# Attention then SwiGLU on one core: another order of loads and work in the opening

## The chip, the core and the metric

The kernel runs on one NeuronCore of a Trainium2 chip. The metric is the device time of one execution in microseconds; a comparison uses the median over several runs. The core has a matrix engine (TensorE, PE in the profile), three engines for elementwise work (VectorE = DVE, ScalarE = ACT, GpSimd = POOL) and SyncE (SP), whose queue issues all data transfers here. Every engine works through its own instructions in order and waits on semaphores for the others. TensorE writes to PSUM, and GpSimd doesn't touch PSUM, so PSUM is read by VectorE and ScalarE alone.

## The reference: what is computed

Causal attention with a sliding window of 64 keys over 8 batches x 8 heads x 576 tokens of 64 features, and a gated feed-forward block on its result (4608 tokens, width 512, inner width 1536):

```python
scores = np.matmul(q, k.transpose(0, 1, 3, 2)) / np.sqrt(64)
rel = pos[:, None] - pos[None, :]
scores = np.where((rel >= 0) & (rel < 64), scores, -1e9)
attn = softmax(scores)                 # over the keys
x = (attn @ v), tokens x (heads * 64)
g = x @ w_gate
out = (g * sigmoid(g) * (x @ w_val)) @ w_out
```

All inputs and the output are float32 in device memory. The kernel casts to bfloat16 for the matmuls and accumulates in float32.

## The kernel before

**Tiling.** The tokens are cut into 36 groups of 128 (`ORDER`, L35). Two groups are a chunk, the unit in which q and k are loaded. Four groups (two chunks) are a tile of 512 tokens, the unit of the feed-forward. The gate and value weights are cut into six slices of 256 inner columns, `weights(s, i)` with i = 0 for gate and 1 for value; slice s serves the inner blocks m = 2s and 2s+1 of 128 columns. `weights_o(s)` loads a sixth of the output weights.

**Attention of a group.** `load` (L85) or `load1` (L95) brings q or k of a chunk, `load_vg` (L104) v of a group. `cast_k` (L122) makes bfloat16 of q or k. `turn2` (L157) transposes it by eight TensorE transposes into PSUM and copies it out to `kT` and `qT`; `turn1` (L149) does the same by two DMA transposes. `keys_before` (L133) copies the last 64 keys of a chunk in front of the next. `cast_v` (L176) makes the two shifted copies of v, `vo` and `ve`. `scores` (L196) is the product of keys and queries, with the mask added by further matmuls where `masked` is set; `weigh` (L221) is the exponential on ScalarE, followed by two VectorE multiplies with the mask where it was not set. `products` (L235) multiplies by v (a 65th column of ones gives the sum), `norm` (L251) divides, `turn_x` (L262) transposes the group's result on TensorE into `xT`, and `turn_x1` (L272) by a DMA transpose.

**Feed-forward.** `cast_w` (L287) casts a weight slice. `step(t, m, c0, n)` (L302) is block m of tile t for the n tokens from c0: four matmuls for the gate, four for the value, then tanh on ScalarE. `finish` (L317) takes the oldest open step and does its two VectorE operations, which give `hT` and release the step's PSUM. There are two PSUM buffers each for gate and value, so a step needs the `finish` of the step two before it. `project(t, s)` (L323) multiplies 128 tokens of `hT` by the output weights in 12 matmuls, evicts on ScalarE and stores. `warm(n)` (L337) issues n matmuls of zeros into a gate buffer; nothing reads them.

**What sets the order.** The kernel is written under a manual schedule: the order of calls in the source is the order of each engine's queue. The opening (L379 to L627) is a list of calls written out one by one: it does the attention of groups 0 to 11, all steps of tiles 0 and 1, the projection of tile 0, and loads all weights. From L631 a loop of regular rounds does the rest; it begins with `step(2, 0)`. A call with engines as arguments, such as `cast_k(0, "q_f", (act, dve))`, puts one half on each named engine.

**Buffers.** Two buffers each for staged q, k and v (`stage`), six for staged weights (`wst`), three each for `kT`, `qT` and the exponentials, four PSUM buffers (`ps_a`) shared by transposes, scores, products and projections. A load waits on SP's queue until its buffer has been cast; all later loads wait behind it. Eight semaphores serve the transfers in turn, so that a transfer also waits for the one eight before it.

Of the kernel before, what the change touches and what calls it, by code (L numbers as in the profile page):

```python
# [17 lines left out]
def kernel(  # L18
# [55 lines left out]
    dve, pool, act, sp = nc.vector, nc.gpsimd, nc.scalar, nc.sync  # L74
# [10 lines left out]
    def load(n, src, nm):  # L85

        x_f = stage.tile([P, H, 2, D], FP32, name=nm, tag=nm)
        ((_, b, s),) = tokens(2 * n)
        sp.dma_start(  # L89
            x_f[:].rearrange("r h c d -> r h (c d)"),  # L90
            src[b, :, s:s + 256, :].rearrange("h (r c) d -> r h (c d)", c=2),
        )
        staged[nm, n] = x_f[:].rearrange("r h c d -> r c h d")
# [28 lines left out]
    def cast_k(n, nm, eng):  # L122
        x_f = staged.pop((nm, n))
        x_b = cast.tile([P, 2, DM], BF16, name=nm + "b", tag=nm + "b")
        y = x_b[:].rearrange("r c (h d) -> r c h d", h=H)
        if isinstance(eng, tuple):
            for c in range(2):
                copy(eng[c], y[:, c], x_f[:, c])
        else:
            copy(eng, y, x_f)  # L130
        words[nm, n] = x_b
# [205 lines left out]
    def warm(n):  # L337
        w_ps = ps_f.tile([P, 512], FP32, name="w_ps", tag="g")
        for _ in range(n):
            nc.tensor.matmul(w_ps[:], wz[:, 0:P], wz[:])  # L340

    def begin():

        dve.memset(wz[:], 0.0)  # L344
        make_identity(nc, identb[:])
        dve.memset(masks[0][:], 1.0)
        dve.memset(minus[0][:], 0.0)
        pool.affine_select(
            out=masks[0][:], in_=masks[0][:], compare_op=ALU.is_ge, fill=0.0,
            base=64, pattern=[[0, 2], [1, 64]], channel_multiplier=-1,  # L350
        )
        pool.affine_select(
            out=masks[0][:], in_=masks[0][:], compare_op=ALU.is_ge, fill=0.0,
            base=-1, pattern=[[0, 2], [-1, 64]], channel_multiplier=1,
        )
        for a in range(2):

            y = minus[0][64 * a:64 * a + 64]
            pool.affine_select(
                out=y, in_=y, compare_op=ALU.is_ge, fill=NEG,  # L360
                base=64, pattern=[[-1, P]], channel_multiplier=1,
            )
            pool.affine_select(
                out=y, in_=y, compare_op=ALU.is_ge, fill=NEG,
                base=-1, pattern=[[1, P]], channel_multiplier=-1,
            )

        pool.tensor_copy(minus[1][:, 64:P], minus[0][:, 64:P])
        pool.memset(minus[1][:, 0:64], NEG)
        pool.tensor_copy(masks[1][:], masks[0][:])  # L370
        pool.memset(masks[1][0:64, 0, :], 0.0)
        for i in (0, 2):
            dve.memset(kT[i][:, :, 0:64], 0.0)
        for i in (0, 4):
            dve.memset(ve[i][0:64], 0.0)
        for x in vo + ve:
            dve.memset(x[:, :, D:VW], 1.0)

    begin()  # L379
    load(0, q, "q_f")  # L380
    load(0, k, "k_f")
    cast_k(0, "q_f", (act, dve))
    load(1, k, "k_f")
    load_vg(0)
    cast_k(0, "k_f", (act, pool))
    load_vg(1)
    warm(11)
    turn2(0, "q_f", (act, dve))
    warm(4)
    turn2(0, "k_f", (act, dve))  # L390
    cast_k(1, "k_f", (dve, act))
    warm(3)
    scores(1)
    load(1, q, "q_f")
    cast_v(0, (dve, pool, pool))
    scores(0, True)
    cast_k(1, "q_f", pool)
    load(2, k, "k_f")
    cast_v(1, (dve, None, None))
    weigh(1)  # L400
    load(2, q, "q_f")
    weigh(0)
    warm(6)
    products(0)
    load_vg(2)
    load_vg(3)
    weights(5, 0)
    load_vg(4)
    norm(0)
    keys_before(1)  # L410
    turn2(1, "k_f", (act, dve))
    warm(4)
    turn_x(0)
    turn2(1, "q_f", (act, dve))
    products(1)
    warm(1)
    scores(2, True)
    cast_k(2, "k_f", pool)
    norm(1)
    cast_k(2, "q_f", dve)  # L420
    weigh(2)
    warm(1)
    scores(3, True)
    weigh(3)
    weights(5, 1)
    load_vg(5)
    turn2(2, "q_f", act)
    load(3, k, "k_f")
    cast_v(2, (dve, pool, pool))
    keys_before(2)  # L430
    turn2(2, "k_f", dve)
    turn_x(1)
    warm(2)
    products(2)
    load(3, q, "q_f")
    norm(2)
    cast_v(3, (act, pool, pool))
    warm(1)
    scores(4, True)
    weights(0, 0)  # L440
    weigh(4)
    products(3)
    norm(3)
    cast_v(4, (act, pool, pool))
    warm(1)
    turn_x(2)
    warm(2)
    turn_x(3)
    weights(0, 1)
    scores(5, True)  # L450
    products(4)
    cast_w(5, 1, pool)
    cast_v(5, pool)
    weigh(5)
    cast_w(5, 0, dve)
    step(0, 10, 0, 256)
    norm(4)
    weights(4, 0)
    step(0, 10, 384, 128)
    turn_x(4)  # L460
    products(5)
    load_vg(6)
    finish()
    keys_before(3)
    cast_k(3, "k_f", (act, pool))
    weights(4, 1)
    norm(5)
    finish()
    step(0, 11)
    cast_k(3, "q_f", (dve, act))  # L470
    load_vg(7)
    turn_x(5)
    turn2(3, "k_f", (dve, act))
    turn2(3, "q_f", (act, dve))
    load(4, k, "k_f")
    cast_w(0, 0, pool)
    finish()
    step(1, 11, 0, 256)
    cast_w(0, 1, act)
    scores(6, True)  # L480
    load(4, q, "q_f")
    finish()
    load_vg(8)
    scores(7)
    step(0, 0)
    weigh(6)
    step(1, 0, 0, 256)
    cast_w(4, 0, pool)
    finish()
    finish()  # L490
    weigh(7)
    cast_w(4, 1, act)
    cast_v(6, pool)
    step(0, 1)
    cast_v(7, (act, pool, pool))
    products(6)
    step(0, 8)
    norm(6)
    cast_k(4, "k_f", (act, pool))
    products(7)  # L500
    turn_x(6)
    finish()
    norm(7)
    weights(3, 0)
    step(0, 9)
    cast_k(4, "q_f", (act, pool))
    cast_w(3, 0, pool)
    weights(1, 0)
    finish()
    weights(3, 1)  # L510
    weights(1, 1)
    keys_before(4)
    load_vg(9)
    finish()
    turn_x(7)
    cast_w(3, 1, pool)
    turn2(4, "k_f", (dve, act))
    turn2(4, "q_f", act)
    step(1, 8)
    finish()  # L520
    step(1, 1)
    weights(2, 0)
    load(5, q, "q_f")
    cast_w(1, 0, pool)
    finish()
    scores(8)
    cast_w(1, 1, pool)
    scores(9)
    weigh(8)
    weights_o(4)  # L530
    load(5, k, "k_f")
    step(1, 10)
    finish()
    cast_w(2, 0, pool)
    step(0, 6)
    keys_before(5)
    weights(2, 1)
    finish()
    step(1, 6)
    finish()  # L540
    step(0, 2)
    weights_o(5)
    cast_k(5, "q_f", pool)
    finish()
    weights_o(1)
    weigh(9)
    step(0, 7)
    cast_v(8, act)
    step(1, 3)
    finish()  # L550
    cast_k(5, "k_f", (act, pool))
    step(1, 9)
    cast_v(9, (dve, pool, pool))
    finish()
    cast_w(2, 1, pool)
    turn2(5, "q_f", act)
    step(0, 3)
    weights_o(2)
    load_vg(10)
    weights_o(0)  # L560
    finish()
    casts_o(1, pool)
    finish()
    step(0, 10, 256, 128)
    products(9)
    casts_o(4, pool)
    products(8)
    step(0, 4)
    norm(9)
    casts_o(5, pool)  # L570
    finish()
    finish()
    turn2(5, "k_f", act)
    cast_v(10, pool)
    load_vg(11)
    step(1, 2)
    norm(8)
    finish()
    weights_o(3)
    step(0, 5)  # L580
    load1(6, k, "k_f")
    casts_o(0, pool)
    load_vg(12)
    finish()
    scores(10)
    load(7, k, "k_f")
    scores(11)
    casts_o(2, pool)
    casts_o(3, dve)
    weigh(11)  # L590
    turn_x1(8)
    keys_before(6)
    weigh(10)
    cast_k(6, "k_f", pool)
    step(1, 7)
    step(1, 11, 256, 256)
    finish()
    turn_x(9)
    project(0, 3)
    cast_v(11, (pool, dve, act))  # L600
    load1(6, q, "q_f")
    turn1(6, "k_f")
    load1(7, q, "q_f")
    finish()
    cast_k(6, "q_f", (act, pool))
    turn1(6, "q_f")
    step(1, 5)
    products(11)
    norm(11)
    products(10)  # L610
    cast_k(7, "k_f", (dve, pool))
    step(1, 0, 256, 256)
    project(0, 0)
    norm(10)
    cast_v(12, (pool, act, act))
    turn_x(10)
    turn_x(11)
    finish()
    project(0, 1)
    load_vg(13)  # L620
    finish()
    project(0, 2)
    load_vg(14)
    keys_before(7)
    step(1, 4)
    turn2(7, "k_f", act)
    load1(8, k, "k_f")  # L627


    dve.memset(vL[:, :, :, D:VW], 1.0)  # L630
# [90 lines left out]
```

The softmax here doesn't subtract the row's maximum and nothing guards it: scores larger than these inputs give would overflow.

## Time and profile before

| | us |
|---|---|
| median of 4 runs | 339.5 |
| lowest to highest | 339.09 to 339.76 |
| profiled execution, its own time | 338.88 |
| its span, first to last instruction | 337.1 |

| engine | busy us | share of the span |
|---|---|---|
| TensorE matmuls | 328.6 | 97% |
| TensorE weight loads | 162.5 | 48% |
| VectorE | 229.1 | 68% |
| ScalarE | 150.9 | 45% |
| GpSimd | 103.0 | 31% |

The transfers moved 56.98 MB, 169 GB/s on the mean of the span; between 50 and 60 us it was 345 GB/s. To read the profile: the busy time of a matmul reaches to the end of its result, and the next one starts before that, so the sums of durations are longer than the time taken; the distance from one start to the next tells the pace. A row with "<-" names what the engine waited for. The `warm` matmuls count as busy.

### The profile page before, as it was taken

The page shows a single profiled execution, that of the slowest core. Times are in us where ns is not written, and L with a number is a line of the kernel's source. Part 1 is how long each engine was busy: PE and PEld are TensorE (multiplying, and loading weights), DVE is VectorE, ACT ScalarE, POOL GpSimd, SP SyncE. Part 2 cuts the span into 40 slices and gives each one's busy share as a digit, 9 for nine tenths or more (in the row PEclk, how much of TensorE's full clock was granted, in tenths as well). Part 3 has the DMA queues.
Part 4 walks back from the last instruction along what each step waited for, and adds up shares of the span by engine and source line. Part 5 has one row for each costly group of instructions (what it writes and reads, how often), then busy time and mean ns, then how long its engine had stood idle before and what let it go on. Part 6 is the DMA issues. An engine that isn't in the chain of part 4 may idle for free.

```text
span 337.1 us, 7312 instructions
## 1 busy us (share of the span) xinstructions
PE 328.6 (97%) x2784; PEld 162.5 (48%) x2784; DVE 229.1 (68%) x486; ACT 150.9 (45%) x266; POOL 103.0 (31%) x150
## 2 busy tenths in 40 slices
PE   8888999999999999999999999999999999999996
PEld 3566554555444444444444444444444444444444
DVE  4777899896476868786767665866765866655520
ACT  4586867465534343434343433334343434233222
POOL 4355555832333333333333333223333110000000
PEclk9999999999999999999999999999999999999999
DMA  8999999969988989998989897899797420211014
GB/s 207 263 263 300 281 326 341 315 130 191 234 176 178 165 177 152 186 169 140 202 149 194 130 200 146 175 167 190 146 195 141 115 64 34 63 33 31 31 47 111
DMA packets 151155, 56.98 MB, mean 169 GB/s; under 512 B 125264, under 2 KB 145104, under 8 KB 151120
## 3 DMA queue, kind: packets, MB, share of 16 engines
q1 hardware_dynamic: 151120, 56.51, 78.3%
q8 instruction: 22, 0.36, 0.5%
q14 instruction: 13, 0.11, 0.1%
HBM read 37.75 MB, written 9.44 MB: 140 GB/s over the span
## 4 chain that ended last, share of the span: by engine, by line
PE 86%; DMA 6%; SPq 3%; DVE 2%; issue 1%; ACT 0%; POOL 0%; ACTq 0%; DVEq 0%; POOLq 0%
PE g_ps L309 27%; PE o_ps L327 26%; PE v_ps L309 26%; PE ao_ps L245 3%; PE s_ps L207 2%; DMA w_f<-in_moe_w_val_dram 2%; DMA v_f<-in_v_dram 2%; SPq L110 2%; DMA kT<-k_fb 1%; PE tp L170 1%; DVE sg L320 1%; SPq L89 1%; DMA out_dram<-os__4939 1%; PE xtp L269 0%; SPq L284 0%
## 5 line engine op out<-in xcount | busy, mean ns | idle before, releaser
L309 PE MATMUL v_ps<-xT,wv 128*128 128x512 bf16 (+1 forms) x448 | 111.6, 371 | 1.5 <-POOL wv L120 1.5
L309 PE MATMUL g_ps<-xT,wg 128*128 128x512 bf16 (+1 forms) x448 | 111.9, 372 | 0.6 <-DVE sg L320 0.6
L320 DVE SCALAR_TENSOR_TENSOR sg<-th,g_ps 128x512 f32<-128x512 f32 (+1 forms) x112 | 74.3, 664 | 55.2 <-ACT th L314 55.1
L314 ACT ACTIVATE th<-g_ps 128x512 f32<-128x512 f32 (+1 forms) x112 | 65.0, 583 | 78.3 <-PE g_ps L309 77.0
L327 PE MATMUL o_ps<-wo,hT 128*128 128x512 bf16 (+2 forms) x456 | 98.5, 368 | 0.0
L321 DVE TENSOR_TENSOR hT<-sg,v_ps 128x512 bf16<-128x512 f32 (+1 forms) x112 | 74.9, 668 | 13.1 <-PE v_ps L309 1.7
L309 PEld LDWEIGHTS <-wv 128*128 128x128 bf16 x448 | 43.4, 98 | 51.6 <-POOL wv L120 1.8
L327 PEld LDWEIGHTS <-hT 128*128 128x128 bf16 x456 | 43.6, 98 | 49.3
L309 PEld LDWEIGHTS <-wg 128*128 128x128 bf16 x448 | 40.9, 98 | 44.0 <-issue 0.8
L227 ACT ACTIVATE E<-s_ps 128x512 bf16<-128x512 f32 x72 | 38.9, 598 | 10.0 <-PE s_ps L207 8.6
L120 POOL CAST q_fb<-q_f 128x1024 bf16<-128x1024 f32 (+1 forms) x15 | 14.8, 988 | 69.9 <-DMA q_f<-in_q_dram 58.2
L120 POOL CAST k_fb<-k_f 128x1024 bf16<-128x1024 f32 (+1 forms) x17 | 16.2, 955 | 60.4 <-DMA k_f<-in_k_dram 50.5
L229 DVE TENSOR_TENSOR E<-E,mask 128x512 bf16<-128x512 bf16 x60 | 29.1, 514 | 7.9 <-ACT E L227 7.2
L120 POOL CAST ve<-v_f 64x512 bf16<-64x512 f32 x49 | 30.9, 630 | 8.5 <-DMA v_f<-in_v_dram 5.7
L256 DVE TENSOR_TENSOR x_b<-ao_ps,r 128x256 bf16<-128x256 f32 x72 | 30.6, 424 | 2.5
L120 POOL CAST vo<-v_f 128x512 bf16<-128x512 f32 x24 | 15.0, 624 | 7.0 <-DMA v_f<-in_v_dram 7.0
L245 PEld LDWEIGHTS <-E 128*64 128x64 bf16 x576 | 11.4, 110 | 8.2 <-issue 5.9
L255 DVE RECIPROCAL r<-ao_ps 128x4 f32<-128x4 f32 x72 | 12.5, 173 | 1.6 <-PE ao_ps L245 1.6
L207 PEld LDWEIGHTS <-kT 64*128 64x128 bf16 x512 | 9.9, 95 | 6.8 <-issue 3.4
L340 PE MATMUL w_ps<-wz 128*128 128x512 bf16 x36 | 11.9, 455 | 1.3 <-DVE wz L344 1.3
L245 PE MATMUL ao_ps<-ve,E 128*64 128x65 bf16 x256 | 12.4, 196 | 0.3
L245 PE MATMUL ao_ps<-vo,E 128*64 128x65 bf16 x256 | 12.5, 196 | 0.0
(99 smaller groups left out, 149.5 us busy)
## 6 DMA issues: line engine op xcount, KB each, us to landing
v_f<-in_v_dram SPq DMA_DIRECT2D x32, 256.0 KB, 4.9
q_f<-in_q_dram SPq DMA_DIRECT2D x20, 256.0 KB, 4.5
k_f<-in_k_dram SPq DMA_DIRECT2D x18, 256.0 KB, 4.2
k_f<-in_k_dram SPq DMA_DIRECT2D x7, 512.0 KB, 7.1
q_f<-in_q_dram SPq DMA_DIRECT2D x6, 512.0 KB, 7.5
w_f<-in_moe_w_gate_dram SPq DMA_DIRECT2D x6, 512.0 KB, 6.3
w_f<-in_moe_w_val_dram SPq DMA_DIRECT2D x6, 512.0 KB, 7.3
wo_f<-in_moe_w_out_dram SPq DMA_DIRECT2D x6, 512.0 KB, 7.7
```

The costliest lines, as they stand in the source:

```text
L120: eng.tensor_copy(y, x)
L207: nc.tensor.matmul(ps[a][:, p, b], keys, qT[g // 2 % QR][y, p, o:o + 64], tile_position=(64 * a, 0), start=True, stop=not masked,)
L227: act.activation(e, x[:], AF.Exp, scale=0.125)
L229: dve.tensor_mul(e, e, mk[:].unsqueeze(1).to_broadcast([P, 4, 2, 64]))
L245: nc.tensor.matmul(o_ps[64 * b:64 * b + 64, i, :], Es[g % ER][:, y, b], z[:, y, :], tile_position=(0, 64 * b),)
L255: dve.reciprocal(r[:], o_ps[:, :, D])
L256: dve.tensor_mul(xb[g][:, 256 * h:256 * h + 256].rearrange("r (y d) -> r y d", y=4), o_ps[:, :, 0:D], r[:].unsqueeze(2).to_broadcast([P, 4 ...
L309: nc.tensor.matmul(ps[:, 0:n], w[:, c, P * m:P * m + P], xT[t][:, c, c0:c0 + n], start=(c == 0), stop=(c == 3),)
L314: act.activation(th[:, 0:n], g_ps[:, 0:n], AF.Tanh, scale=0.5)
L320: dve.scalar_tensor_tensor(sg[:, 0:n], th[:, 0:n], 1.0, g_ps[:, 0:n], ALU.add, ALU.mult)
L321: dve.tensor_mul(hT[t][:, m, c0:c0 + n], sg[:, 0:n], v_ps[:, 0:n])
L327: nc.tensor.matmul(o_ps[:, a:b], hT[t][:, c, P * s:P * s + P], wo[:, c, a:b], start=(c == 0), stop=(c == 11),)
```

## The change

Only the list of calls in the opening is replaced; functions, buffers and the loop stay. In words:

- The first loads are k0, q0, k1, v0, q1, v1, v2, v3 (before: q0, k0, k1, v0, v1, q1, then k2, q2, v2, v3). Then come the four transfers of weight slices 5 and 0, and only after them k2, q2, v4, v5, slice 4, k3, q3, v6 and slice 2.
- TensorE does the attention of groups 0 to 3, turns their results, and runs the first tile's steps on block 11 (first half), block 10 (two halves) and block 0 before it transposes k2 and q2. Before, it did the attention of groups 0 to 4 ahead of its first step.
- The engines of many casts are other ones, and more steps are split into halves.
- `scores(7)` is masked by matmuls. Group 8 is turned on TensorE and not by DMA; q of chunk 6 is turned on TensorE at the end of the opening and k of chunk 7 by DMA (before, the other way round).
- `warm` matmuls: 36 before, 33 after.
- In the last part q6 is issued behind the store of `project(0, 0)`, and v13 behind that of `project(0, 3)`.

The diff, cut to what is spoken of:

```diff
     begin()
+    load(0, k, "k_f")
     load(0, q, "q_f")
-    load(0, k, "k_f")
-    cast_k(0, "q_f", (act, dve))
     load(1, k, "k_f")
     load_vg(0)
-    cast_k(0, "k_f", (act, pool))
-    load_vg(1)
-    warm(11)
-    turn2(0, "q_f", (act, dve))
-    warm(4)
-    turn2(0, "k_f", (act, dve))
-    cast_k(1, "k_f", (dve, act))
-    warm(3)
-    scores(1)
-    load(1, q, "q_f")
-    cast_v(0, (dve, pool, pool))
-    scores(0, True)
-    cast_k(1, "q_f", pool)
-    load(2, k, "k_f")
...
-    load(2, q, "q_f")
-    weigh(0)
-    warm(6)
-    products(0)
-    load_vg(2)
-    load_vg(3)
-    weights(5, 0)
-    load_vg(4)
...
-    cast_w(5, 1, pool)
-    cast_v(5, pool)
-    weigh(5)
-    cast_w(5, 0, dve)
-    step(0, 10, 0, 256)
-    norm(4)
-    weights(4, 0)
-    step(0, 10, 384, 128)
...
+    cast_k(0, "q_f", (dve, act))
+    cast_k(0, "k_f", pool)
+    warm(11)
+    turn2(0, "k_f", (act, dve))
+    load(1, q, "q_f")
+    warm(3)
+    turn2(0, "q_f", (act, dve))
+    warm(3)
+    scores(0, True)
+    scores(1)
+    load_vg(1)
+    cast_k(1, "k_f", (act, dve))
+    cast_v(0, (pool, act, dve))
+    load_vg(2)
+    load_vg(3)
+    cast_v(1, pool)
+    weigh(1)
+    weights(5, 0)
+    weigh(0)
+    warm(7)
+    turn2(1, "k_f", act)
+    weights(5, 1)
+    cast_k(1, "q_f", dve)
+    keys_before(1)
+    turn2(1, "q_f", act)
+    products(0)
+    norm(0)
+    cast_v(2, (pool, pool, act))
+    warm(4)
+    products(1)
+    scores(2, True)
+    norm(1)
+    weights(0, 0)
+    weights(0, 1)
+    load(2, k, "k_f")
+    scores(3, True)
+    cast_v(3, (pool, dve, act))
+    load(2, q, "q_f")
+    weigh(2)
+    weigh(3)
+    turn_x(0)
+    cast_w(5, 0, pool)
+    warm(1)
+    products(2)
+    warm(2)
+    products(3)
+    norm(2)
+    norm(3)
+    turn_x(1)
+    turn_x(2)
+    load_vg(4)
+    load_vg(5)
+    cast_w(5, 1, pool)
+    warm(2)
+    step(0, 11, 0, 256)
+    finish()
+    cast_w(0, 0, pool)
+    cast_w(0, 1, dve)
+    turn_x(3)
+    keys_before(2)
+    step(0, 10, 0, 256)
+    finish()
+    cast_k(2, "k_f", (dve, pool))
+    step(0, 10, 256, 256)
+    finish()
+    weights(4, 0)
+    step(0, 0)
+    weights(4, 1)
+    load(3, k, "k_f")
+    cast_k(2, "q_f", (act, dve))
+    turn2(2, "k_f", (dve, act))
+    turn2(2, "q_f", (dve, act))
+    step(0, 11, 256, 256)
+    finish()
+    keys_before(3)
+    cast_v(4, (pool, pool, act))
+    scores(5, True)
+    cast_v(5, (pool, dve, act))
+    load(3, q, "q_f")
+    weigh(5)
+    scores(4, True)
+    weigh(4)
+    cast_w(4, 0, pool)
+    finish()
+    step(0, 1)
+    products(5)
+    load_vg(6)
+    cast_w(4, 1, act)
+    products(4)
+    norm(5)
+    weights(2, 0)
+    step(0, 8)
...
+    weights(2, 1)
+    load_vg(7)
+    finish()
+    weights(1, 0)
+    step(1, 8, 0, 256)
+    scores(7, True)
+    finish()
+    cast_w(2, 0, act)
+    weights(1, 1)
+    scores(6, True)
+    cast_v(6, pool)
+    weigh(7)
+    cast_w(2, 1, dve)
+    step(1, 10, 0, 256)
...
+    turn_x(8)
...
+    project(0, 0)
+    load(6, q, "q_f")
+    load_vg(12)
+    project(0, 2)
...
+    turn1(6, "k_f")
...
+    turn1(7, "k_f")
...
+    project(0, 3)
+    step(1, 11, 256, 256)
+    load_vg(13)
+    turn2(6, "q_f", (dve, act))
```

## The prediction

> **What bounds the kernel now.** I read the page's engine rows and slices first, then the costliest groups, then the chain of waits, then the timelines of TensorE and GpSimd in the first 45 us.
>
> ```profile
> span 337.1 us, 7312 instructions
> PE 328.6 (97%) x2784; PEld 162.5 (48%) x2784; DVE 229.1 (68%) x486; ACT 150.9 (45%) x266; POOL 103.0 (31%) x150
> ...
> PE   8888999999999999999999999999999999999996
> ...
> PEclk9999999999999999999999999999999999999999
> DMA  8999999969988989998989897899797420211014
> ...
> L309 PE MATMUL v_ps<-xT,wv 128*128 128x512 bf16 (+1 forms) x448 | 111.6, 371 | 1.5 <-POOL wv L120 1.5
> ...
> L340 PE MATMUL w_ps<-wz 128*128 128x512 bf16 x36 | 11.9, 455 | 1.3 <-DVE wz L344 1.3
> ```
>
> TensorE is below 9 tenths only in the first four slices (34 us) and the last. Outside the opening the time is matmuls back to back, so an edit of the opening moves the end only by what it changes in the opening: TensorE work, and time in which TensorE idles or runs `warm`, which computes nothing. The DMA row is near full as well: data paces the opening.
>
> The chain of waits, then TensorE's timeline (start us, duration us, engine, line, operation, count, idle before it):
>
> ```profile
> 18.00 7.36 DMA w_f<-in_moe_w_val_dram
> ...
> 25.48 1.04 POOL wv L120
> ```
>
> ```profile
> 1.26 4.78 PE L340 MATMUL w_ps<-wz 128*128 128x512 bf16 x11 [1.26 <-DVE wz L344]
> ...
> 24.44 0.61 PE L309 MATMUL g_ps<-xT,wg 128*128 128x256 bf16 x4
> 26.57 0.61 PE L309 MATMUL v_ps<-xT,wv 128*128 128x256 bf16 x4 [1.52 <-POOL wv L120]
> ...
> 28.21 1.04 PE L309 MATMUL g_ps<-xT,wg 128*128 128x512 bf16 x4
> ...
> 87.70 0.61 PE L170 MATMUL tp<-identb,k_fb 128*128 128x128 bf16 x8
> 88.15 1.03 PE L309 MATMUL g_ps<-xT,wg 128*128 128x512 bf16 x4
> ```
>
> The value slice of `weights(5,1)` lands at 25.4 and holds the first feed-forward step. From 28.21 TensorE runs almost without a gap; the loop (L631) begins at 88.15.
>
> GpSimd's timeline gives landings, since its casts wait for them:
>
> ```profile
> 16.10 1.04 POOL L120 CAST k_fb<-k_f 128x1024 bf16<-128x1024 f32 x1 [2.01 <-DMA k_f<-in_k_dram]
> ...
> 31.27 1.04 POOL L120 CAST wg<-w_f 128x1024 bf16<-128x1024 f32 x1 [2.15 <-DMA w_f<-in_moe_w_gate_dram]
> 34.34 1.04 POOL L120 CAST wg<-w_f 128x1024 bf16<-128x1024 f32 x1 [2.04 <-DMA w_f<-in_moe_w_gate_dram]
> 35.57 0.62 POOL L120 CAST vo<-v_f 128x512 bf16<-128x512 f32 x1 [0.18 <-DMA v_f<-in_v_dram]
> ...
> 38.22 0.61 POOL L120 CAST ve<-v_f 64x512 bf16<-64x512 f32 x1 [0.69 <-DMA v_f<-in_v_dram]
> ...
> 40.06 0.61 POOL L120 CAST k_fb<-k_f 128x512 bf16<-128x512 f32 x1 [0.56 <-DMA k_f<-in_k_dram]
> ```
>
> Two weight slices lie between 31.27 and 34.34: 1.53 us each. v takes 1.23 (34.34 to 35.57), k or q 1.8 (38.22 to 40.06).
>
> **What the opening does besides waiting.** From one start to the next in the timeline: a full step 1.73 us (28.21 to 29.94), a half 0.88, a quarter 0.44, eight transposes of `turn2` 0.445, `turn_x` 0.22, masked scores 0.48, plain 0.29, products 0.32, `project` 2.59.
> - Before, up to 88.15: steps 41.6, six masked and six plain scores 4.6, products 3.8, thirteen `turn2` 5.8, eleven `turn_x` 2.4, four projects 10.4: 68.7. So 19.45 us are idle or `warm`. Counted up to 28.21 the work is 9.7: 18.5 lost there, 0.95 later.
> - After: `scores(7)` is masked too (+0.19; it saves VectorE two multiplies), `turn_x(8)` takes the place of a DMA transpose (+0.22), three more steps are split (+0.1): 69.2, so +0.5. `turn2` stays thirteen: q of chunk 6 comes to TensorE, k of chunk 7 leaves it. `warm` falls from 36 to 33, 3 x 0.216 = 0.65, but it is filler and counts only as lost time.
>
> **The loads in their new order.** k0, q0, k1, v0 land as before (5.0, 6.8, 8.7, 9.9); q1 and v1 swap and are both there at 12.9, as now. Then v2, v3, four weight slices, k2, q2. At the prices above: v3 15.4, `weights(5,0)` 16.9, (5,1) 18.4, (0,0) 19.9, (0,1) 21.5, k2 23.3, q2 25.1. The trace is slower than such a sum: from 12.94 to q3 at 29.86 it moved 4 k/q, 4 v and 2 slices, 15.2 by these prices against 16.9, a slip of 1.8 (mostly k2, 3.2 us behind q1). For the first 12 of those us I add half of it at q2 and less before: (5,1) at 18.9, (0,1) 22.1, k2 24.1, q2 25.9, v5 28.4, `weights(4,1)` 31.5. The slip is the unknown: 0 to 1.8 by this row, and more if the bytes alone count (below).
>
> Here a rule may be weighed. "DMA: Bandwidth & Descriptors" (Specifications; Bandwidth) puts line rate at runs of 512 B and more, and the HBM limit at about 358 GB/s. The slices (1 KB runs) do 343, but k and q, with 512 B runs, only 291, and v 213. By the rule q2 would land near 23, 2 us sooner; I take the rows.
>
> **TensorE through the new opening**, each queue in program order:
> - k0's cast moves whole to GpSimd (1.04 instead of 0.6 on two engines), and q0 lands second: scores begin at 8.75, as now (8.70). ScalarE now has v0's cast (9.9 to 10.5) ahead of `weigh(1)`, so both weighs end at 12.65, not 11.35; the k1 and q1 copies follow (13.65, 14.65), products(0) come at 13.2 instead of 11.05 under seven `warm`, scores(2) at 14.8, scores(3) at 16.0 behind `norm(1)`. Weighs 2 and 3 end at 18.2, x of groups 0 and 1 is turned at 19.7. This path loses some 2 us against now, under cover of the slices, which land at the same time.
> - First step (0,11, half): gate part 19.75, value part 20.0 after GpSimd's cast of (5,1), 18.9 + 1.04. Now: 24.44 and 26.57. But only 5.5 us of other work is done by then (now 7.9).
> - (0,10) in two halves runs to 22.5. `cast_w(0,1,dve)` stands on VectorE ahead of the `finish` that frees the PSUM pair: 22.1 + 0.7, `keys_before(2)` 0.35, first half of `finish` 0.42: step (0,0) starts at 23.6, 1.1 us idle, and ends at 25.3. The k2 cast on VectorE holds the next `finish`, too, until 25.3.
> - `turn2(2,q)` waits for q2: 25.9 + 0.62 cast; 0.8 us idle. Then half of (0,11), scores 5 and 4. ScalarE, which had to wait for q2, does copies, two v casts and four exponentials before it gets to the tanh of (0,1) and the cast of `weights(4,1)`: products(4) wait 0.6, step (0,8)'s value part 0.4. `turn_x(4)` starts at 34.0.
> - Work done by 34.0: 16.9, lost 17.1. Before, at equal work, 18.75 was lost. From here slices 2, 1, 3 land ahead of their steps (VectorE is the closest: a `finish` of a full step is 1.37 us against 1.73 of matmul, plus 1.2 for each norm); I find 0.4 us at step (1,10) and else the short gaps of now, 0.2 us more.
>
> **Later edits with one answer: nothing.** On SP, q6 goes behind the store of project(0,0) and v13 behind that of project(0,3). q6 is needed by the last `turn2`, v13 by products(13) in the loop's first round, both some 8 us after issue; v lands in 4.9 (median). Without that cover each would cost its landing, about 5. Output slices: same bytes as now before the first project (71 us), where six `wo` casts end at 70.5 now; cover about 1 us, and the DMA row is down to 6 in that slice. The DMA transposes of k6 and k7 (2.5 us) lie under the projects.
>
> **Sum.** 18.75 - 17.1 = 1.65 gained, less 0.5 of work, less 0.2: about -0.95. Profiled execution 338.88 (span 337.1, the rest around it unchanged): 337.9. The median of the runs is 339.5, 0.6 above it: **338.5 us**.
>
> One rule speaks against this. "TensorE: Matmul & The Clock Gate" (Why this matters for your kernels) wants no TensorE gap above some 3 us, or the clock halves. The first 11 `warm` take 0.43 us each and later ones 0.216, though the clock row shows 9 throughout, so the halving exists here. The change has fewer `warm` and longer waits, but none above 1.2 us, and the present wait of 1.5 us at 26.57 is followed by a half step at full pace. I cost it at zero; at half clock for 3.4 us (estimate from that page) it would be +1.7, and the change would lose.
>
> **Rivals.**
> - *The wait moves from the weight slice to q2 (slower).* If landing follows bytes and not kinds, q2, which ends 6.0 MiB, lands when the twelfth half-megabyte lands now, k3's: by 28.4 (ScalarE casts it at 28.37). TensorE is in order, so 2.5 us later than taken, one for one: -0.95 + 2.5 = +1.55, 341.0. It decides from q2 at 26.85. For it: k2's 3.2 us now, and VectorE standing behind (0,1) and k2. Against: the slices are quicker per byte.
> - *An exchange of waits.* Full slip of 1.8 at q2: 26.8, change 0: 339.5.
> - *Clean landings.* No slip, q2 at 25.1: 0.8 less, until ScalarE's chain binds: 337.7. The stretch from 31 to 42 us runs like this now.
>
> **Chances and range.** Forecast 0.43, clean landings 0.12, exchange 0.16, late q2 0.29. Some 0.2% (0.7 us) is what a measurement can tell from no change; so faster 0.55, same 0.16, slower 0.29. The forecast alone spans 337.7 to 339.2; clean landings reach 337.0, late q2 341.0 and a little over: 337.0 to 341.3 leaves out a tenth at each side.
>
> **What would show it.** Right: first gate step near 20, its value part within 1 us; step (0,0) waiting for VectorE about 1 us; `turn2(2,q)` at 26.5; loop start at 87.2. Wrong: q2 landing after 26.85, a TensorE gap over 1.5 us between 20 and 45, first matmuls after a gap at 0.43 us, or a loop that isn't as full as now.

## The result, and the profile after

| | before | after |
|---|---|---|
| median | 339.64 us (55 runs) | 338.16 us (36 runs) |
| lowest to highest | 338.45 to 340.92 | 337.06 to 340.48 |
| ratio, 95% interval | | 0.9961, 0.9951 to 0.997 |
| profiled execution | 338.88 | 337.57 |
| its span | 337.1 | 335.9 |
| start of the loop | 88.15 | 87.51 |
| from there to the end of the span | 249.0 | 248.3 |

The changed kernel is faster by 1.48 us between the medians; 338.5 was forecast, and 338.16 was measured. Measured twice more, beside fresh runs of the kernel before, the same file gave ratios of 0.9987 (0.997 to 1.0005) and 0.998 (0.9955 to 1.0004), which is 0.3 and 0.5 us between the medians. So the sign is the same each time, but of the three intervals only the first excludes no change. The size lies between 0.3 and 1.5 us, and why it isn't firmer is part of what follows.

The page of the changed kernel, its engine rows, slices and the costliest groups:

```profile
span 335.9 us, 7388 instructions
PE 326.9 (97%) x2825; PEld 164.3 (49%) x2825; DVE 226.6 (67%) x491; ACT 151.8 (45%) x268; POOL 100.4 (30%) x148
...
PE   7888999999999999999999999999999999999996
PEclk9999999999999999999999999999999999999999
DMA  7999999979968999798979698989787520211013
...
L309 PE MATMUL v_ps<-xT,wv 128*128 128x512 bf16 (+1 forms) x460 | 112.1, 366 | 0.4 <-DVE r L255 0.4
```

The slices look as before: four slices of a TensorE that isn't full, then a full one. The last row has changed most: the value matmuls had waited 1.5 us for a weight cast, and now 0.4 us. The same is seen in the chain of waits, which no longer goes through a weight slice but through q of chunk 2:

```profile
16.89 9.58 DMA q_f<-in_q_dram
26.49 0.63 ACT q_fb L118
...
27.16 0.62 PE tp L170 x8
```

TensorE's timeline (start us, duration us, engine, line, operation, count, idle before it):

```profile
20.95 0.60 PE L309 MATMUL g_ps<-xT,wg 128*128 128x256 bf16 x4
21.38 0.60 PE L309 MATMUL v_ps<-xT,wv 128*128 128x256 bf16 x4
...
24.07 1.02 PE L309 MATMUL g_ps<-xT,wg 128*128 128x512 bf16 x4
25.79 0.61 PE L170 MATMUL tp<-identb,k_fb 128*128 128x128 bf16 x8
27.16 0.62 PE L170 MATMUL tp<-identb,q_fb 128*128 128x128 bf16 x8 [0.77 <-ACT q_fb L118]
...
33.66 1.04 PE L309 MATMUL v_ps<-xT,wv 128*128 128x512 bf16 x4 [0.43 <-DVE r L255]
...
87.51 1.03 PE L309 MATMUL g_ps<-xT,wg 128*128 128x512 bf16 x4
```

The first feed-forward step stands at 20.95 instead of 24.44, and its value part follows at once. The transposes of q2 wait 0.77 us. From 33.66 on there is hardly a gap. The row at 33.66 names a `norm`, because that ended last. What `step(0, 8)` needed there was ScalarE's cast of `weights(4, 1)`, from 32.56 to 33.60, and the weight loads of the same matmuls (PEld) name it:

```profile
33.66 0.55 PEld L309 LDWEIGHTS <-wv 128*128 128x128 bf16 x4 [0.93 <-ACT wv L118]
```

GpSimd's casts give the landings, as before:

```profile
19.56 1.04 POOL L120 CAST wv<-w_f 128x1024 bf16<-128x1024 f32 x1 [0.45 <-DMA w_f<-in_moe_w_val_dram]
...
24.32 0.61 POOL L120 CAST k_fb<-k_f 128x512 bf16<-128x512 f32 x1 [2.29 <-DMA k_f<-in_k_dram]
```

Of the 1.3 us by which the span is shorter (337.14 and 335.85), the opening gave 0.64 and the loop, in which nothing was edited, 0.65. TensorE in the kernel before has two short waits there, which the changed kernel does not have. Its timeline before:

```profile
209.78 1.02 PE L309 MATMUL g_ps<-xT,wg 128*128 128x512 bf16 x4 [0.43 <-DVE sg L320]
...
260.92 1.02 PE L309 MATMUL g_ps<-xT,wg 128*128 128x512 bf16 x4 [0.18 <-DVE sg L320]
```

Behind each of them stands a copy on VectorE that waits for the DMA transposes of a k. For the first it is this one; the `finish` that TensorE waits for starts behind it, at 209.05:

```profile
208.71 0.43 DVE L145 COPY kL<-kT 128x1024 bf16<-128x1024 bf16 x1 [3.78 <-DMA kT<-k_fb]
```

The waits of this copy, summed over the execution (us in total, times, longest), of the kernel before:

```profile
DVE kL L145 <- DMA kT<-k_fb: 7.3, 2, 3.8
```

and of the changed kernel:

```profile
DVE kL L145 <- DMA kT<-k_fb: 5.4, 2, 3.4
```

VectorE waits 1.9 us less for the same transposes of the same loop, in two waits, and TensorE has no wait at those places.

### The profile page after: what moved, and what is told of

Its sections match the earlier page's. It is cut to its first block, busy times and chain, and to the rows that moved or that the text cites. A ratio compares the mean times of both kernels' runs of the same rounds, so it can differ in the third digit from the quotient of the medians.

```text
span 335.9 us, 7388 instructions
## 1 busy us (share of the span) xinstructions
PE 326.9 (97%) x2825; PEld 164.3 (49%) x2825; DVE 226.6 (67%) x491; ACT 151.8 (45%) x268; POOL 100.4 (30%) x148
## 4 chain that ended last, share of the span: by engine, by line
PE 90%; DMA 6%; SPq 3%; ACT 1%; DVE 1%; issue 0%; ACTq 0%
PE g_ps L309 28%; PE v_ps L309 27%; PE o_ps L327 27%; PE ao_ps L245 3%; DMA q_f<-in_q_dram 3%; PE s_ps L207 3%; DMA v_f<-in_v_dram 2%; SPq L110 1%; SPq L89 1%; PE tp L170 1%; DMA out_dram<-os__4994 1%; PE xtp L269 1%; DVE x_b L256 0%; PE s_ps L215 0%; ACT q_fb L118 0%
## 5 line engine op out<-in xcount | busy, mean ns | idle before, releaser
L314 ACT ACTIVATE th<-g_ps 128x512 f32<-128x512 f32 (+1 forms) x115 | 65.8, 572 | 76.5 <-PE g_ps L309 73.6
L309 PEld LDWEIGHTS <-wv 128*128 128x128 bf16 x460 | 44.7, 98 | 49.3 <-ACT wv L118 0.9
L309 PEld LDWEIGHTS <-wg 128*128 128x128 bf16 x460 | 41.8, 98 | 42.2 <-issue 0.6
L120 POOL CAST q_fb<-q_f 128x1024 bf16<-128x1024 f32 x13 | 13.8, 1061 | 66.0 <-DMA q_f<-in_q_dram 33.6
L229 DVE TENSOR_TENSOR E<-E,mask 128x512 bf16<-128x512 bf16 x58 | 23.7, 434 | 9.3 <-ACT E L227 8.6
L120 POOL CAST ve<-v_f 64x512 bf16<-64x512 f32 x47 | 28.8, 613 | 2.9
L120 POOL CAST vo<-v_f 128x512 bf16<-128x512 f32 x30 | 19.0, 633 | 29.1 <-DMA v_f<-in_v_dram 28.9
L207 PE MATMUL s_ps<-qT,kT 64*128 64x64 bf16 x512 | 12.2, 191 | 0.4 <-DVE x_b L256 0.3
L120 POOL CAST vL<-v_f 64x512 bf16<-64x512 f32 x15 | 9.5, 636 | 10.0 <-DMA v_f<-in_v_dram 9.2
```

What stands on the lines that cost most here:

```text
L120: eng.tensor_copy(y, x)
L207: nc.tensor.matmul(ps[a][:, p, b], keys, qT[g // 2 % QR][y, p, o:o + 64], tile_position=(64 * a, 0), start=True, stop=not masked,)
L229: dve.tensor_mul(e, e, mk[:].unsqueeze(1).to_broadcast([P, 4, 2, 64]))
L309: nc.tensor.matmul(ps[:, 0:n], w[:, c, P * m:P * m + P], xT[t][:, c, c0:c0 + n], start=(c == 0), stop=(c == 3),)
L314: act.activation(th[:, 0:n], g_ps[:, 0:n], AF.Tanh, scale=0.5)
```

## The experiments

**Theory.** The gain of the opening comes from the two slices that are loaded early together with steps that need only the attention of groups 0 to 3; the price is that q2 lands late, and from there each microsecond of its lateness is one of the kernel. **Rivals.** The place of the loads alone is the gain; or q2 needn't be late; or the `warm` matmuls and the TensorE clock decide; or the first step, which came 1.2 us later than forecast, is what costs. Not undone one by one were the engines of the casts, the masking of `scores(7)`, and the places of q6 and v13.

### Both kernels again

> The kernel before, unchanged, for a second profile. The question is what the two gaps in the loop are (0.43 us at 209.8 and 0.24 at 260.9 in the first profile, where a VectorE copy of keys waits for a DMA transpose). If they belong to this order of work, they are there again, some 0.6 us in sum, and the span from the loop's first step to the end is 248.9 to 249.0. If they are an accident of one execution, that span is 248.4, as in the profile of the changed kernel. The opening should end at 88.1 to 88.2 either way.

> The changed kernel, unchanged, for a second profile and as the yardstick of this call. 0.995 to 0.997 of the time before. The opening ends at 87.3 to 87.7, q of chunk 2 lands at 26.0 to 27.0. If the loop of the changed kernel is free of gaps by its order of work, the rest takes 248.4 again; if by accident, gaps of 0.2 to 0.6 us appear.

> The change a third time, unaltered, in more rounds. If the lateness of q2 scatters from execution to execution of one and the same kernel, its median lies between those of the first two measurements, 338.2 and 338.9, so a ratio of 0.996 to 0.999, and the span of its times is again wider than that of the kernel before. In its profile, the loop start minus 87.51 should be the start of the ScalarE cast of q2 minus 26.49, within 0.3 us. Rival (the second measurement was another chip with another pace): the lateness in this profile does not answer to its loop start.

The kernel before, one execution: 338.82, span 337.1, loop start 88.23, and the larger wait of the loop is there again (0.42 at 209.85); near 260.9, where some 0.2 was expected, there is none over 0.15. So the larger wait belongs to the program and not to one execution, and from loop start to the end it is 248.9 (249.0 in the first profile).

The change, second measurement: 338.89 (337.88 to 340.45), ratio 0.9987, where 0.995 to 0.997 was expected. In its profile the span is 337.3 and the loop starts at 88.99. TensorE's timeline of it:

```profile
24.41 1.02 PE L309 MATMUL g_ps<-xT,wg 128*128 128x512 bf16 x4 [0.80 <-DVE sg L320]
...
28.65 0.62 PE L170 MATMUL tp<-identb,q_fb 128*128 128x128 bf16 x8 [0.88 <-ACT q_fb L118]
```

The cast of q2 is at 27.98 instead of 26.49, 1.49 later, and the loop starts 1.48 later: one for one.

The change, third: 338.84 (337.66 to 341.27), ratio 0.998. The cast of q2 is at 27.38, 0.89 later than in the first profile, but the loop starts at 89.78, 2.27 later. The expectation that q2 alone tells the loop start fell, by 1.4 us. TensorE's timeline has where the rest went:

```profile
28.05 0.62 PE L170 MATMUL tp<-identb,q_fb 128*128 128x128 bf16 x8 [0.89 <-ACT q_fb L118]
...
43.10 1.04 PE L309 MATMUL v_ps<-xT,wv 128*128 128x512 bf16 x4 [0.58 <-DVE wv L120]
...
50.93 0.62 PE L170 MATMUL tp<-identb,q_fb 128*128 128x128 bf16 x8 [0.20 <-POOL q_fb L120]
```

and VectorE's, what the second of these waits for, `weights(2,1)`:

```profile
42.35 0.69 DVE L120 CAST wv<-w_f 128x1024 bf16<-128x1024 f32 x1 [0.90 <-DMA w_f<-in_moe_w_val_dram]
```

Compared start by start with the first profile, the distance grows from 0.95 to 1.68 at this value part, to 1.9 behind it, where the next slices are late too, and to 2.26 at the q transposes, and stays. So the lateness of any load of the opening is paid for, q2's first. Over the six profiles with this order of loads (three of the change, three of its edits below) the loop starts 61.0 to 62.4 us behind the cast of q2: q2 sets the least that is paid, and not the whole. As expected, the times spread more than those of the kernel before in all three measurements (3.4 us from lowest to highest against 2.5, 2.6 against 1.6, and 3.6 against 3.3).

Part of the lateness is there early. SyncE's queue has it (start us, duration us of the issue), first in the first profile, then in the second:

```profile
11.35 1.02 SPq L284 DMA_DIRECT2D w_f<-in_moe_w_gate_dram  x1
12.42 2.27 SPq L284 DMA_DIRECT2D w_f<-in_moe_w_val_dram  x1
```

```profile
11.37 2.39 SPq L284 DMA_DIRECT2D w_f<-in_moe_w_gate_dram  x1
13.80 0.84 SPq L284 DMA_DIRECT2D w_f<-in_moe_w_val_dram  x1
```

The issue of the gate slice of 5 takes 1.02 or 2.39 us, and so the value slice is issued at 12.42 or 13.80. Of the six profiles, the two with the earliest q2 (cast at 26.31 and 26.49) have it at 12.46 and 12.42, and the four with a later q2 at 13.68 to 13.80. What holds this issue isn't shown, and it doesn't set how late q2 comes (26.93 to 28.49).

### One part of the change alone: the slices early

In the kernel before, the two transfers of slice 5 go ahead of k2 and q2; the order of the work stays.

```diff
     cast_k(1, "q_f", pool)
+    weights(5, 0)
+    weights(5, 1)
     load(2, k, "k_f")
...
     load_vg(3)
-    weights(5, 0)
     load_vg(4)
...
     weigh(3)
-    weights(5, 1)
     load_vg(5)
```

> The kernel before with one part of the change: the two transfers of weight slice 5 are issued ahead of k2 and q2 (and so ahead of v2, v3), and the order of the work on the engines stays. Theory (the gain is the pair of early slices and steps that need no more attention than that of groups 0 to 3): slice 5 lands by 19, but the first step stands in TensorE's queue behind the transposes of k2 and q2 and all work of group 4, and q2 comes 3 us later than now (17.8), so turn2(2,q) waits about 3 us at 18.43; of this, the value part's wait of 1.5 us at 26.57 is won back. Loop start 89 to 90.5, 340.3 to 341.8. Rival (early slices by themselves are the gain): loop start at or under 87.7, 338.0 to 339.0.

342.12 (341.6 to 343.28), ratio 1.008 (1.0053 to 1.0108), loop start 92.11. TensorE's timeline:

```profile
21.77 1.03 PE L170 MATMUL tp<-identb,q_fb 128*128 128x128 bf16 x8 [4.12 <-DVE q_fb L120]
...
29.77 0.61 PE L309 MATMUL g_ps<-xT,wg 128*128 128x256 bf16 x4
30.22 0.60 PE L309 MATMUL v_ps<-xT,wv 128*128 128x256 bf16 x4
```

The value part no longer waits for its slice, but the transposes of q2 wait 4.12 us in front of everything, and the first step comes 5.3 us later than in the kernel before. The loads' place alone is not the gain; it needs the work that can be done without q2. (The place isn't quite that of the change: here v2 and v3 come behind slice 5 as well, and land at 21.9 and 23.0 instead of 18.7 and 19.6. The long wait in front is q2's.) The loss is larger than expected. q2 was cast at 21.02, about as late as thought, but behind the long wait the granted clock was 0.50 from 22 to 26 us, and the eight transposes take 1.03 us instead of 0.62.

### The other part undone: q2 early

In the change, k2 and q2 are issued ahead of the slices (first diff), or even ahead of v2 and v3 (second); nothing else is moved.

```diff
     load_vg(3)
+    load(2, k, "k_f")
+    load(2, q, "q_f")
     cast_v(1, pool)
...
     weights(0, 1)
-    load(2, k, "k_f")
     scores(3, True)
     cast_v(3, (pool, dve, act))
-    load(2, q, "q_f")
```

```diff
     load_vg(1)
+    load(2, k, "k_f")
+    load(2, q, "q_f")
     cast_k(1, "k_f", (act, dve))
...
     weights(0, 1)
-    load(2, k, "k_f")
     scores(3, True)
     cast_v(3, (pool, dve, act))
-    load(2, q, "q_f")
```

> The changed kernel with only the slices held back: k and q of chunk 2 stand between v3 and the weight slices, so that v2 and v3 land as with the change (unlike the run that put them ahead of v2, where v2 itself came 3.3 us later). Theory (the gain is the slices landing before k2 and q2): value slice 5 lands at 22.5 to 23.5 instead of 19.6, slice 0 at 25.5 to 26.5, the first step's value part at 24, step (0,0) at 27; the opening ends 1.5 to 3 us after the 87.5 of the change, and the time is 1.000 to 1.005 of the kernel before. Rival (an exchange of waits): within 0.5 us of the changed kernel.

> The changed kernel with one part undone: k and q of chunk 2 are loaded ahead of v2, v3 and the weight slices again; all else stays. Theory (the gain is the earlier slices): the slices land some 3.6 us later, the first step's value part moves from 21.4 to 24 to 25, step (0,0) waits for its own slice until 27 to 28 and q2 waits for nothing; the opening ends 1.5 to 3 us later than with the change, 1.002 to 1.006 of the time before. Rival (the gain is the other engines for the casts and the shorter filler, and the order of loads is an exchange of one wait for another): within 0.5 us of the changed kernel, 0.995 to 0.998.

Ahead of the slices: 341.54 (341.23 to 342.44), ratio 1.007 (1.0043 to 1.0096), loop start 91.25. TensorE's timeline:

```profile
22.23 0.61 PE L309 MATMUL g_ps<-xT,wg 128*128 128x256 bf16 x4 [1.78 <-POOL wg L120]
23.70 0.61 PE L309 MATMUL v_ps<-xT,wv 128*128 128x256 bf16 x4 [0.85 <-POOL wv L120]
...
27.96 1.02 PE L309 MATMUL g_ps<-xT,wg 128*128 128x512 bf16 x3 [1.68 <-DVE sg L320]
```

All waits are now waits for slices (the third through the cast of `weights(0,1)` at 26.75 on VectorE), 4.3 us in sum against 0.3 + 0.77 in the change. That is what the early slices are worth in this order of work: 3.7 us at the loop start against the first profile of the change, and 1.5 and 2.3 against the other two, where 1.5 to 3 had been expected. The granted clock was full in this profile; in two of the four executions its mean was 0.990 and 0.994, so the median holds some of that too.

Ahead of v2 and v3: 342.24, ratio 1.008 (1.0058 to 1.0102), loop start 92.10. Here v2 came late as well (18.8 instead of 15.5), and TensorE's timeline has one long wait and a slow first step behind it:

```profile
20.85 0.58 PE L269 MATMUL xtp<-identb,x_b 128*128 128x128 bf16 x4 [3.90 <-ACT E L227]
...
25.59 1.06 PE L309 MATMUL g_ps<-xT,wg 128*128 128x256 bf16 x4
26.45 0.97 PE L309 MATMUL v_ps<-xT,wv 128*128 128x256 bf16 x4
```

So this run mixes two causes, a late v2 and a slow clock, and the run before it is the cleaner one.

### q2 between the slices, and the first step earlier

Of the slices only 5 stays ahead of q2; slice 0 goes behind it, and `step(0, 0)`, which needs it, goes with its casts behind the scores of groups 5 and 4. In a second kernel, the exponentials of groups 2 and 3 also go ahead of the third copy of v3, which had held them until 17.11. In a third, this last edit is made alone in the change.

```diff
-    weights(0, 0)
-    weights(0, 1)
     load(2, k, "k_f")
...
     turn_x(2)
+    weights(0, 0)
+    weights(0, 1)
     load_vg(4)
...
-    step(0, 0)
+    turn2(2, "k_f", (dve, act))
...
+    scores(4, True)
     weigh(5)
-    scores(4, True)
     weigh(4)
+    step(0, 0)
```

```diff
     scores(3, True)
-    cast_v(3, (pool, dve, act))
     load(2, q, "q_f")
     weigh(2)
     weigh(3)
+    cast_v(3, (pool, dve, act))
```

> The changed kernel with k2 and q2 between slice 5 and slice 0, and with step (0,0) behind the turns of k2 and q2 and scores 5 and 4, so that nothing stands in front of data that lands later. If the wait for q2 is what the change still pays (one us of landing is one us of the end), q2 lands at 23 to 24 and holds nothing, slice 0 holds step (0,0) at 26.5 to 27.5, and step (0,1) starts 0.3 to 1 us earlier than with the change; 0.993 to 0.997 of the time before. If it only hands the wait to slice 0, within 0.3 us of the change.

> As the run before it in this call, and ScalarE does the exponentials of groups 2 and 3 ahead of the third copy of v3, which is needed only in the loop. In the changed kernel ScalarE waits 0.4 us for v3 there, and TensorE waits 0.9 for the exponential at 17.75. The first step moves up by 0.3 to 0.9 until the value slice of 5 holds it; since slice 0 then holds step (0,0), at most 0.4 us of it reaches the end: 0.992 to 0.997.

> The change with the exponentials of groups 2 and 3 on ScalarE ahead of the third copy of v3, which held them until 17.1. They would start at 16.1 or a little later, so x of groups 0 and 1 is turned 1 us earlier and the first gate half could start at 20.0 or so. Theory (q2's landing holds the end of the opening, so that time won before it is only waited longer): loop start minus cast of q2 as in the change (61.0), the time unchanged within 0.3 us. Rival (the first step's lateness of 1.2 us costs time): 0.5 to 1 us faster than the change's runs beside it.

The first: 338.68 (337.88 to 340.89), ratio 0.9987 (0.9968 to 1.0007), where the change itself gave 0.9987 and 0.998 in its second and third measurement. TensorE's timeline shows the wait handed on in pieces: the q2 transposes come 1.4 us sooner, and then wait for their casts and copies, because `step(0, 0)` no longer stands between.

```profile
25.76 0.28 PE L170 MATMUL tp<-identb,q_fb 128*128 128x128 bf16 x2 [0.45 <-ACT q_fb L118]
26.63 0.51 PE L170 MATMUL tp<-identb,q_fb 128*128 128x128 bf16 x6 [0.59 <-DVE q_fb L120]
27.70 0.20 PE L207 MATMUL s_ps<-qT,kT 64*128 64x64 bf16 x2 [0.56 <-DVE qT L120]
```

The second: 339.15, ratio 0.9993 (0.9973 to 1.0013), where 0.992 to 0.997 was expected. The first gate part is at 20.17, but its value part waits 0.83 us for slice 5 and starts at 21.60, later than in the change. The 1.2 us by which the first step was late are covered by the slice.

The third: 338.63 (337.47 to 340.18), ratio 0.9972 (0.995 to 0.9994), beside 0.998 for the change on the same chip; the two intervals overlap almost wholly, so no gain of the edit is shown. Its profile is of a late execution (340.18), and has something else to show, TensorE's timeline:

```profile
20.07 0.60 PE L309 MATMUL g_ps<-xT,wg 128*128 128x256 bf16 x4
21.69 0.61 PE L309 MATMUL v_ps<-xT,wv 128*128 128x256 bf16 x4 [1.03 <-POOL wv L120]
...
26.30 0.42 PE L309 MATMUL g_ps<-xT,wg 128*128 128x512 bf16 x1 [2.03 <-DVE sg L320]
26.94 1.06 PE L309 MATMUL g_ps<-xT,wg 128*128 128x512 bf16 x2 [0.22 <-issue]
27.79 1.91 PE L309 MATMUL v_ps<-xT,wv 128*128 128x512 bf16 x4
29.50 0.81 PE L170 MATMUL tp<-identb,k_fb 128*128 128x128 bf16 x8
30.15 0.61 PE L170 MATMUL tp<-identb,q_fb 128*128 128x128 bf16 x8
```

Again the early gate part only waits for the value slice. Then the cast of `weights(0,1)` is at 25.09 (it was at 23.20 and 23.09 in the second and third measurement of the change), TensorE idles 2.03 us, and the four value matmuls of `step(0, 0)` take 1.91 us for 1.03. The busy time by windows (us, busy time of each engine, granted clock, DMA share, GB/s) has the granted clock:

```profile
22.00:26.00 4.00, 2.27 (x23) 1.91 (x22) 1.33 (x4) 1.25 (x3) 1.04 (x1) 1.00 0.80 211
26.00:30.00 4.00, 3.48 (x13) 1.66 (x14) 2.28 (x6) 1.22 (x2) 1.38 (x2) 0.57 0.78 175
```

From 26.30 to the k2 transposes at 29.50 is 3.2 us for a step of 1.73. The cast of q2 is at 28.49, so its transposes could have started at 29.16 (0.67 after the cast, as in the change); they start at 30.15. So the clock costs 1 us on the path (an estimate from these starts), and 0.7 of it is left at the loop start, which is 61.71 behind the cast of q2, not 61.02.

### The clock, and the filler

The change without the `warm` matmuls behind the first eleven (22 of them).

```diff
-    warm(3)
...
-    warm(3)
...
-    warm(7)
...
-    warm(4)
...
-    warm(1)
...
-    warm(2)
...
-    warm(2)
```

> The changed kernel without its 22 later filler matmuls; the first 11 stay. They write nothing that is read, so the result is whole. If idle gaps of up to some 2.5 us cost no clock, the time is that of the changed kernel within 0.3 us, since every filler stands in front of a wait. If the clock halves, first matmuls after the gaps take 0.43 us each, the attention before 20 us and the first steps run late, and the time is 0.7 to 3 us above the changed kernel.

338.08 (337.29 to 339.31), ratio 0.9969 (0.9954 to 0.9984), beside 0.9987 (0.997 to 1.0005) for the change on the same chip: not slower, and, since the intervals overlap, not shown to be faster. (A time 0.8 us under the change's stood in neither case of the expectation.) The halving came, by windows:

```profile
14.00:18.00 4.00, 3.79 (x98) 3.03 (x94) 2.88 (x9) 3.44 (x6) 3.75 (x6) 0.50 1.12 325
18.00:22.00 4.00, 3.68 (x47) 2.87 (x47) 2.15 (x8) 2.35 (x6) 2.05 (x3) 0.50 1.12 331
22.00:26.00 4.00, 4.00 (x31) 2.94 (x29) 3.42 (x9) 1.82 (x5) 0.73 (x2) 0.90 1.20 264
```

The first gate part takes 1.01 us instead of 0.60. Yet `step(0, 0)` follows at 24.60 (24.07 in the change), and the transposes of q2 stand at 26.99, right behind the cast at 26.31: the slow matmuls lie in time that TensorE would have waited. (The loop starts at 87.86, 0.35 later than in the first profile of the change, because the transposes of q3 wait 0.69 us for their cast at 37.56.) In three kernels above the clock fell when work already stood waiting behind TensorE; for the last of them the price is worked out, 1 us, for the other two it isn't told apart from the waits.

The mean granted clock is on record for every execution of the change, the profiled and the others. In 8 of the 58 executions of the change it is 0.994 or 0.995, and these took 339.43 to 341.27 us; in the other 50 it is full to within 0.001, and none of them took more than 339.76. The execution with the wait of 2.03 us, at 0.995 as well, shows what such a mean stands for: 0.5% of 338 us is 1.7 us, or 3.4 us at half clock. The kernel before has 3 such executions of 28 in the third measurement (340.67 to 341.58) and none of 19 in the second. So every time of the change above 339.76 is of an execution that lost clock, whether or not q2 was late in it; which wait brought it on isn't shown where there is no profile.

### Where the loop's waits come from

The loop is the same text in both kernels. In the opening the kernel before issues one transfer more (group 8's transpose), so that in the loop each transfer meets another one of the eight semaphores. Two kernels shift this by one: the kernel before with x of group 8 turned on TensorE, and the change with it turned by DMA.

```diff
-    turn_x1(8)
+    turn_x(8)
```

```diff
-    turn_x(8)
+    turn_x1(8)
```

> The kernel before with one edit at the end of the opening: group 8 is turned on TensorE, as in the change, and not by a DMA transpose. The question is what the loop's gaps (0.42 us at 209.8 and some 0.2 at 260.9, in both profiles of the kernel before and in none of four with the new opening) come from. If from the number of transfers before the loop (each waits for the one eight before it, on eight semaphores in turn, and this edit makes the count equal to the change's), they are gone; if from what else the opening leaves, they stay. The opening ends at 88.4, 0.2 later.

> The change with x of group 8 turned by a DMA transpose, as before, and not on TensorE: 0.22 us of TensorE work less and one SP transfer more (240 as before, instead of 239), so that in the loop every transfer meets the semaphore that it met in the kernel before. Theory A (the short gaps of the loop near 210 and 261, seen in the kernel before and not in the change, come from how the loop's transfers fall on the eight semaphores): they come back, 0.3 to 0.6 us in all from loop start to the end, 0.1 to 0.4 slower than the change. Theory B (they come from something else in what the old opening leaves): no gaps, and the time as in the change or 0.2 us less.

The kernel before with one transfer fewer: 340.5 in one execution, loop start 89.95 (TensorE waits 0.68 us for the exponential of group 8 at 70.58, and later work with it). One wait of the loop is still there, 0.36 us at 262.57, the one near 210 isn't. The change with one more: 338.8 (338.33 to 339.62), ratio 0.9981 (0.9967 to 0.9996), as the change beside it, and no wait in the loop. So the count of transfers by itself isn't the cause. The time from loop start to the end of the span, over all profiles:

| opening | profiles | loop start | from there to the end |
|---|---|---|---|
| before, and two edits of it | 4 | 88.15 to 92.11 | 248.8 to 249.5 |
| the change, and edits of it | 10 | 87.51 to 92.10 | 248.3 |

It isn't the time at which the loop starts either, since both rows span the same. The kernel with the slices early, which has the old order of work, has the largest waits of all, 0.53 and 0.39 us. It is something that the old list of calls leaves behind, and in which the list of the change differs in any of its variants. Which, stays open: what differs besides is which k and q of the last chunks are turned by DMA, and how the buffers stand at the loop's start; neither was tried.

## Why the prediction came out right, and where it did not

**Right: what bounded the opening, and the exchange.** The value slice no longer holds TensorE, and q2 does, as the chain shows. `weights(5,1)` was taken to land at 18.9 and was cast at 19.56, k2 24.1 and 24.32, q2 25.9 and 26.49; the q2 transposes stood at 26.5 and came at 27.16. The wait of `step(0, 8)` for its value part was 0.4 and is 0.43, and it is for the cast that was named. The late edits with one answer, nothing, cost nothing that can be seen in the first profile: TensorE has no wait from 45 to 90 us. (In the change with group 8 turned by DMA it waits 0.47 us at 73.28 for the cast of an output slice.)

**Right in its place, wrong in its size: the first step.** The gate part was put at 19.75 and came at 20.95: v3 landed at 16.6, not 15.4, and ScalarE's copy of it held the exponentials until 17.11. The 1.1 us of idle before `step(0, 0)` shrank to 0.3 for that reason, so that the step came only 0.5 later than forecast. The kernel with the early exponentials alone showed that this lateness isn't worth anything by itself: the step then waits for its value slice.

**Wrong: the size of the opening's gain.** The sum had 0.95 us for it; the profiled pair has 0.64. In that pair q2 was cast at 26.49 and not 25.9, and 0.3 of these 0.6 us are left at the loop start (87.51 for 87.2). In the other two profiles of the change the loop starts at 88.99 and 89.78, later than in the kernel before (88.15 and 88.23). Over medians, the whole change is worth 0.3 to 1.5 us. If 0.6 of that is the loop, as in the profiles, -0.3 to 0.9 are left for the opening (an estimate), so that only the first measurement speaks for a gain there. The step that failed is the slip of the loads: taken as 0 to 1.8 us for q2 with half of it as the likely value. The profiles with the load order of the change have the cast of q2 at 26.31, 26.49, 26.93, 27.38, 27.98 and 28.49. So the rivals "exchange of waits" and "late q2" (28.4, one for one) aren't other cases of the kernel but other executions of it and of the edits that keep its loads, and the text gave one case for what is a spread. Two of its own signs of being wrong came in them: q2 after 26.85 in four of the six profiles, and a TensorE gap of 2.03 us in one. What makes a load land 2 us later in one execution than in another isn't shown by any run here; the traces only show that the issue of a slice already differs, at 12.4 or 13.7 us.

**Wrong: a loop without change.** The prediction added up the opening alone and took the loop as equal. It gave 0.65 us, half of what the profiled pair differs by, and no step of the prediction had a reason for it. That the total of -0.95 lies between the measured -0.3 and -1.5 is thus in part luck: a gain that was not foreseen stood in for one that was overrated.

**The clock rule.** It was costed at zero, and for the first profile of the change this was right: the clock is full once the first `warm` are through. But it isn't zero in late executions: 8 of 58 lost clock, and the kernel with the early exponentials idled 2.03 us and ran at 0.57 for 4 us, 1 us lost on the path. The Trainium skill, "TensorE: Matmul & The Clock Gate" (Why this matters for your kernels) has gaps of about 3 us and more as the danger. Here 1.52 us (the kernel before) and 1.78 us (q2 ahead of the slices) left the clock alone, 2.03 us did not, in a stretch in which TensorE was busy for 2.27 of 4 us. The measurement decides: in this opening, with thin work, 2 us were enough.

**Landings by bytes or by kind.** The prediction took the rows against the line-rate rule, which it had at q2 near 23 (a sum that takes v at line rate too, though its runs are 256 B; with v at 1.23 us it would be 24.2, an estimate). All six profiles, with q2 at 26.3 to 28.5, are on the side of the rows, and the later ones beyond them.

## What to carry to other kernels

An early load is worth something only together with work that needs nothing else: the slices early with the old order of work lost 2.8 us, the new order of work with the slices late lost 2.3, and both together lost nothing and gained 0.3 to 1.5, some 0.6 of it in the loop. A load that is put last in such a queue can collect the delays of those before it (q2 was cast at 17.7 to 17.8 ahead of the slices, and at 26.3 to 28.5 behind them), so its landing should be given a spread and not a value, and the work that waits for it belongs behind whatever else can be done. Sum a forecast over the whole span, and look in the unchanged part for waits that may come or go.

## What was not expected of the hardware

- The same load of the same program is cast at 26.49, 27.38 or 27.98 us, and the times of the program follow, by 1 to 2 us; the kernel before casts its q2, which is issued ahead of the slices, at 17.68 and 17.80 in two executions.
- The granted clock fell to half after 2.03 us of idle TensorE, and without the filler also between 14 and 22 us, where no single wait is over 1.6 us (11.14, for an exponential) and the work is many small matmuls. At half clock eight transposes took 1.03 to 1.06 us for 0.61, and four matmuls of 256 columns 1.01 to 1.06 for 0.60.
- An untouched loop changed by 0.65 us with the opening in front of it, through DMA transposes: in the SyncE queue of the kernel before, the pair of x transposes at 201.22 takes 3.52 us to issue, in the change 2.56 at 201.18. The four profiles with the old opening have 3.07 to 3.71 for this pair, and nine of the ten with the new one 2.56 or 2.57 (the one without filler 3.18).
